# HGRN2 attention and a low-rank mixer on one core: the first batch's low rank in two groups of columns, and another order of loads around the last unit

## The chip, the cores and the metric

The kernel runs on 1 core of one Trainium2 chip. The metric is the device time of one execution in microseconds (us); lower is better. The profile, the chains and the timelines come from one profiled execution of the kernel.

## The reference

Two blocks follow each other, in float32 (the mixer's weights arrive as float64). For each of 4 batches and 8 heads (768 steps, head size 48) a gated linear recurrence is computed; the heads' outputs side by side make x, and a mixer works on it.

```python
f = 1 / (1 + exp(-f_logit))
for t in range(768):
    state = f[t][:, None] * state + k[t][:, None] * v[t][None, :]
    y[t] = q[t] @ state
x = heads of y side by side            # (4, 768, 384)
u = x + V.T @ (U.T @ x)                # along the sequence: U 768 x 32, V 32 x 768
out = u + relu(u @ w_ch1) @ w_ch2      # 384 -> 1536 -> 384
```

## The kernel before

**Units.** Two heads of one batch make a unit; there are HP = 4 units a batch and 16 in all. A unit takes a 96-column share of x (two heads of 48). `prepare(n)` makes the pieces of a unit's front: gates (f is transposed by TensorE and put through a sigmoid), keep (a scan on VectorE), keys, read_back (a second scan), queries. `attend(n)` makes those of its rear: kept, states (the ds matmuls), scan, scores (sc), read (the y matmuls from the states, L824), inner (the y matmuls within a chunk, L842, and the ScalarE copy of y into x, L848).

**Order.** TensorE (PE), VectorE (DVE) and ScalarE (ACT) run in the order in which the pieces are called; this order is written out by hand. The loop at L928 runs over the four units of the first batch and calls a front and a rear in turn. After it come the last unit's read and inner, then the first batch's mixer: low_rank (U.T x, tile ph, L172), added_up (the four 32-row groups of ph are summed by a matmul with `blocks`, L180), mix (V.T h added to x, tile pu, L197), turn (x transposed, tile put, L207), then the first large matmuls (pz, L219). `busy(n)` issues n matmuls whose result nobody reads (tile idle, L923).

**Loads.** All DMAs are issued by SyncE (SP), whose queue a scheduler orders by the calls and the waits of each. `load(n, names)` brings a unit's operands: f, k and q go into fixed tiles, `late` for even units and `other` for odd ones, each in two DMAs of 144 KB made of pieces of 192 bytes; v goes into one of three v_nat buffers with one DMA of 144 KB and two of 72 KB. `follow`, called as soon as a unit's f, k or q has been read, loads the same operand of unit n + 2 (for the first batch, units 2 and 3; units 4 and 5 are excepted). The loop's end adds the rest:

```python
            if n < 2:
                load(n + 2, "v")
            if n == 1:
                for start, _ in weights[: early + 2]:
                    start()
            elif n > 1:
                load(n + 2, "f", "k", "q", "v")
```

Each entry of `weights` is a pair: `start` issues the DMA of 8-byte values and `end` converts them to float32 (two ACT operations, three of DVE, one of POOL, L90 to L95). The first `early` = 3 are U and V (in two parts), then come twelve pieces of w1, the first FIRST = 6 of which land in spare zw tiles by `place`, the others in one of RAW = 4 w_raw buffers, and twelve of w2. `ahead_by(n, loads)` makes calls of which each starts the load n places further on and ends its own. The ends are called between the mixer's pieces; from piece EARLY on, pieces of the next batch's units are called between them too.

Of the kernel before, what the change touches and what calls it, by code (L numbers as in the profile page):

```python
# [10 lines left out]
F32 = mybir.dt.float32  # L11
U32 = mybir.dt.uint32
U64 = mybir.dt.uint64
I32 = mybir.dt.int32
AF = mybir.ActivationFunctionType
ALU = mybir.AluOpType
AX = mybir.AxisListType

WP = 384

RAW = 4
# [80 lines left out]
def ahead_by(n, loads):  # L102


    def call(i):
        if i + n < len(loads):
            loads[i + n][0]()
        loads[i][1]()

    return [lambda i=i: call(i) for i in range(len(loads))]  # L110
# [36 lines left out]
class Mixer:  # L147
# [6 lines left out]
    def __init__(self, tc, b, x, U, V, w1, w2, sums, ident, blocks, out, two, three, zp, ps_big, ps_mm, wide=False,  # L154
                 z_all=None, room=None, pair=0):
        nc = tc.nc
        P = nc.NUM_PARTITIONS
        NCH, DM = x.shape[1], x.shape[2]
        R, FF = U.shape[2], w1.shape[2]
        NG = P // R  # L160
        NDC, NFC = DM // P, FF // P
# [3 lines left out]
        uT, z, h, S = {}, {}, {}, {}  # L165

        def low_rank():
            pm = ps_mm.tile([P, 512], F32, name="ph", tag="mm")

            for c in range(NCH):  # L170
                g = slice((c % NG) * R, (c % NG + 1) * R)
                nc.tensor.matmul(pm[g, 0:DM], lhsT=U[:, c, :], rhs=x[:, c, :],  # L172
                                 start=(c < NG), stop=(c >= NCH - NG))
            h[0] = two.tile([P, DM], F32, name="h", bufs=1)
            nc.scalar.copy(h[0], pm[:, 0:DM])

        def added_up():

            pm = ps_mm.tile([P, 512], F32, name="ph", tag="mm")
            nc.tensor.matmul(pm[:, 0:DM], lhsT=blocks, rhs=h[0], start=True, stop=True)  # L180
            h[1] = two.tile([P, DM], F32, name="h", bufs=1)
            nc.scalar.copy(h[1], pm[:, 0:DM])

        def add(*args):

            with tc.high_priority(offset=AHEAD):
                nc.vector.tensor_tensor(*args)  # L187

        pu = {}

        def mix(t):

            s = t % 2
            if s == 0:
                pu[0] = ps_big.tile([P, 2, 512], F32, name="pu", tag="big")
            g = slice((t % NG) * R, (t % NG + 1) * R)
            nc.tensor.matmul(pu[0][:, s, 0:DM], lhsT=V[g, t // NG, :], rhs=h[1][g, :], start=True, stop=True)  # L197
            if s == 1:
                add(x[:, t - 1 : t + 1, :], x[:, t - 1 : t + 1, :], pu[0][:, :, 0:DM], ALU.add)

        def turn(a):

# [231 lines left out]
def factored_path(ctx, tc, q, k, v, f_logit, moe_U, moe_V, moe_w_ch1, moe_w_ch2, out, ok):  # L434
# [4 lines left out]
    nc = tc.nc  # L439
    B, H, S, D = q.shape  # L440
    P = nc.NUM_PARTITIONS
    C = P // 2
    NCH = S // C

    NBL = S // P
    HP = H // 2
    DM = H * D
    R = moe_U.shape[1]
    FF = moe_w_ch1.shape[1]
    NDC = DM // P  # L450
    NFC = FF // P
# [15 lines left out]
    two = ctx.enter_context(tc.tile_pool(name="two", bufs=2))  # L467
    three = ctx.enter_context(tc.tile_pool(name="three", bufs=3))
    zp = ctx.enter_context(tc.tile_pool(name="zp", bufs=3))
    ps_big = ctx.enter_context(tc.tile_pool(name="ps_big", bufs=3, space=bass.MemoryType.PSUM))  # L470
# [8 lines left out]
    raw = [{nm: t[:, i, :] for i, nm in enumerate("fkq")} for t in (late, other)]  # L479
# [11 lines left out]
    def load(n, *names):  # L491

        b, hp = divmod(n, HP)
        for nm in names:
            if nm == "v":
                v_tiles[n] = three.tile([P, NBL, 2, D], F32, name="v_nat")
            for par in range(2):
                head = src[nm][b, 2 * hp + par]
                if nm == "v" and par:

                    for s in range(2):
                        nc.sync.dma_start(
                            out=v_tiles[n][(1 - s) * C : (2 - s) * C, :, par, :],
                            in_=head.rearrange("(c s p) d -> s p c d", s=2, p=C)[s],
                        )
                    continue
                if nm == "v" or n < TURNED:
                    dst = v_tiles[n] if nm == "v" else nat[n % 2][nm]
                    nc.sync.dma_start(out=dst[:, :, par, 0:D], in_=head.rearrange("(c p) d -> p c d", p=P))  # L509
                    continue  # L510
                head = head.rearrange("(c i) d -> i c d", i=NB)
                for part in range(2):
                    p0 = par * PAD + part * NB
                    n_ch = min(NB, D - part * NB)
                    nc.sync.dma_start(
                        out=raw[n % 2][nm][p0 : p0 + NB, :].rearrange("p (c d) -> p c d", d=NB)[:, :, 0:n_ch],
                        in_=head[:, :, part * NB : part * NB + n_ch],
                    )
# [9 lines left out]
    blocks = const.tile([P, P], F32, name="blocks")  # L528
# [33 lines left out]
    table = one.tile([P, 1], F32, name="table")  # L562
# [4 lines left out]
    U = const.tile([P, NBL, R], F32, name="U")  # L567
    V = const.tile([P, (NBL * R + P - 1) // P, P], F32, name="V")
    take_in = weight_loader(nc, two, nc.sync)
    weights = [take_in(U, moe_U.rearrange("(c p) r -> p c r", p=P))]  # L570
    weights += [take_in(*pair) for pair in by_rows(V, moe_V, R)]
    early = len(weights)
    w1_rows = moe_w_ch1.rearrange("(c p) f -> p c f", p=P)

    spare = []

    def place():
        if not spare:
            t = zp.tile([P, NFC // 2, 2 * P], F32, name="zw").rearrange("p i t -> p (i t)").bitcast(U64)
            spare.extend([t[:, 0:WP], t[:, WP : 2 * WP]])  # L580
        return spare.pop(0)

    FIRST = 6
    weights += [
        take_in(w1[:, :, i * P : (i + 1) * P], w1_rows[:, :, i * P : (i + 1) * P], place if i < FIRST else None)
        for i in range(NFC)
# [96 lines left out]
    def mixer(b):  # L683
        return Mixer(tc, b, x_tiles[b], U, V, w1, w2, sums if b else None, ident, blocks, out, two, three, zp, ps_big, ps_mm,
                     b == 0, z_all, room if b >= B - 2 else None, FEWER - (b - B + 2) * NCH // 4)
# [180 lines left out]
    def rear(n, *names):  # L866

        if not 0 <= n < NU:
            return []
        if n not in here:  # L870
            here[n] = dict(zip(("kept", "states", "scan", "scores", "read", "inner"), attend(n)))
        return [here[n].pop(nm) for nm in names if nm in here[n]]
# [43 lines left out]
    with tc.manual_schedule(engines={nc.vector.engine, nc.scalar.engine}):  # L916


        idle = ps_mm.tile([P, 512], F32, name="idle", tag="mm")

        def busy(n):
            for _ in range(n):
                nc.tensor.matmul(idle[:, 0:DM], lhsT=ident, rhs=ends[:, 0:DM], start=True, stop=True)  # L923

        busy(1)
        for piece in front(0, "gates"):
            piece()
        for n in range(HP):  # L928
            pieces = front(n, "keep", "keys") + rear(n - 1, "scan", "scores")
            pieces += [lambda: busy(3)] + rear(n, "kept") + front(n, "read_back", "queries")  # L930
            if n + 1 < HP:
                pieces += front(n + 1, "gates") + rear(n - 1, "read", "inner") + rear(n, "states")
            else:
                pieces += rear(n, "states") + rear(n - 1, "read") + rear(n, "scan", "scores") + rear(n - 1, "inner")
            for piece in pieces:
                piece()
            if n < 2:
                load(n + 2, "v")
            if n == 1:


                for start, _ in weights[: early + 2]:
                    start()
            elif n > 1:
                load(n + 2, "f", "k", "q", "v")
        for start, _ in weights[early + 2 : early + FIRST]:
            start()
        loads = ahead_by(early + FIRST, weights)
        for piece in rear(HP - 1, "read") + loads[:2] + rear(HP - 1, "inner") + loads[2 : early + 1]:
            piece()  # L950
        loads = loads[early + 1 :]

        m = mixer(0)
        start = m.before[:5] + m.firsts[0:1] + m.before[5:]
        idles = {1: 1, 2: 1}

        EARLY = 9
        second = chain(front(HP, "gates", "keep", "keys", "read_back", "queries"), steps(HP, 2 * HP + 1))
        for i, (_, piece) in enumerate(start + m.firsts[1:]):
            busy(idles.get(i, 0))  # L960
            piece()
            if loads and i != 1:
                loads.pop(0)()
            if i >= EARLY:
                next(second)()
        for f in loads:
            f()
        n = len(m.seconds) // (NBL // 2)
        todo, after = m.seconds[:-n], m.seconds[-n:]

        attention(second, 12 + 10 * HP - (len(start) + len(m.firsts) - 1 - EARLY), todo)
        m = start_mixer(1, after)
        for f in to_sum:
            f()
    for b in range(2, B - 1):
        todo, after = m.main, m.after
        attention(steps(b * HP + 1, (b + 1) * HP + 1), 10 * HP, todo)
        m = start_mixer(b, after)

    pieces = beside(steps((B - 1) * HP + 1, NU + 1), 10 * (HP - 2), [lambda i=i: sum_of_w(i) for i in range(len(W_SUMS))])  # L980
# [374 lines left out]
```

## Time and profile before

| | us |
|---|---|
| median of 14 runs | 490.58 (488.65 to 494.15) |
| the profiled execution | 490.05 |
| its span | 488.3 |
| PE busy in the span | 471.3 (97%) |
| DVE busy | 356.2 (73%) |
| ACT busy | 163.6 (34%) |
| POOL busy | 36.4 (7%) |
| first large matmul of the mixer (pz) starts at | 57.31 |
| HBM read | 28.70 MB |

The page divides the span into 40 slices of 12.2 us and gives each engine's busy tenths in each. Its chain follows the work that ended last back from the end. A busy PE is not PE at its peak: a matmul's duration also depends on the clock that was granted to it, which the page shows in tenths (PEclk). "Issue" is time in which an engine waited for nothing that the profile shows.

### The profile page before, as it was taken

The numbers are of one execution on the slowest core, as the hardware profiler recorded it, in microseconds if no ns is written. First come the engines' busy times: TensorE is split into PE (matmuls) and PEld (weight loads), VectorE is DVE, ScalarE is ACT, GpSimd is POOL, SyncE is SP. The second block draws the span as 40 slices with busy tenths as digits, with TensorE's granted clock in tenths as the row PEclk, the third lists the DMA queues.
The fourth block names the chain that finished last, engine by engine and source line by source line (L and its number), as shares of the span: only waits on it lengthen the run. The fifth ranks groups of instructions, "written<-read, shape, count | busy, mean of one in ns | idle before, by whom it ended". The sixth has DMA issues, their size and how long they took to land.

```text
span 488.3 us, 12681 instructions
## 1 busy us (share of the span) xinstructions
PE 471.3 (97%) x5519; PEld 400.4 (82%) x5519; DVE 356.2 (73%) x561; ACT 163.6 (34%) x307; POOL 36.4 (7%) x49
## 2 busy tenths in 40 slices
PE   7897999999999999999999999999999999999995
PEld 4675588886666568899899888898979999999995
DVE  5886789778998757656857448796896886958642
ACT  3444575654443313424231403432231312112200
POOL 3001255442000000000000000000000000000000
PEclk9998899999999999999999999999999999999999
DMA  9988976675778512333434100100000000000001
GB/s 145 159 175 157 260 181 154 158 155 66 110 108 128 91 37 33 56 44 79 66 52 85 34 17 17 27 3 20 18 2 0 34 2 16 17 1 34 0 34 38
DMA packets 158679, 34.34 MB, mean 70 GB/s; under 512 B 149206, under 2 KB 157078, under 8 KB 158614
## 3 DMA queue, kind: packets, MB, share of 16 engines
q1 hardware_dynamic: 158614, 33.44, 37.3%
q8 instruction: 45, 0.74, 0.6%
q14 instruction: 20, 0.16, 0.1%
HBM read 28.70 MB, written 4.72 MB: 68 GB/s over the span
## 4 chain that ended last, share of the span: by engine, by line
PE 90%; DVE 3%; DMA 2%; SPq 2%; issue 1%; ACT 1%; DVEq 0%; ACTq 0%
PE pw L273 26%; PE pz L219 23%; PE pp L371 11%; PE po L244 10%; PE y L824 3%; PE y L842 3%; PE sc L749 3%; PE ds L786 2%; PE pt L621 2%; PE put L207 2%; PE pt L770 1%; PE idle L923 1%; SPq L509 1%; PE pu L197 1%; PE ph L172 1%
## 5 line engine op out<-in xcount | busy, mean ns | idle before, releaser
L219 PE MATMUL pz<-uT,w 128*128 128x256 f32 x504 | 115.8, 384 | 0.1
L219 PEld LDWEIGHTS pz<-uT,w 128*128 128x128 f32 x504 | 93.3, 190 | 13.3 <-issue 0.3
L273 PE MATMUL pw<-w,z_all 128*128 128x192 f32 x216 | 37.7, 329 | 0.0
L273 PE MATMUL pw<-zw,w_raw 128*128 128x192 f32 x216 | 37.4, 327 | 0.0
L273 PEld LDWEIGHTS pw<-zw,w_raw 128*128 128x128 f32 x216 | 35.2, 190 | 0.8 <-issue 0.6
L273 PEld LDWEIGHTS pw<-w,z_all 128*128 128x128 f32 x216 | 35.0, 190 | 0.7
L655 DVE TENSOR_TENSOR_SCAN late<-fz,late 128x768 f32<-128x768 f32 x16 | 28.1, 1756 | 9.8 <-ACT fz L650 5.1
L95 POOL TENSOR_TENSOR w<-w_y,w_r 128x384 int32<-128x384 int32 x24 | 30.2, 1258 | 37.0 <-DVE w_y L94 30.0
L229 ACT ACTIVATE z_all<-pz 128x512 f32<-128x512 f32 x33 | 19.7, 596 | 39.6 <-PE pz L219 39.5
L371 PE MATMUL pp<-v_nat,late 128*128 128x128 f32 x224 | 28.8, 275 | 0.0
L673 DVE TENSOR_TENSOR_SCAN late<-fz,other 128x768 f32<-128x768 f32 x16 | 27.9, 1746 | 0.1
L371 PEld LDWEIGHTS pp<-v_nat,late 128*128 128x128 f32 x224 | 27.0, 192 | 0.0
L244 PE MATMUL po<-w,zw 128*128 128x384 f32 x72 | 25.6, 499 | 0.0
L244 PE MATMUL po<-w,z_all 128*128 128x384 f32 x72 | 25.3, 496 | 0.0
L364 ACT ACTIVATE other<-other 128x512 f32<-128x512 f32 x18 | 11.3, 631 | 40.0 <-DVE other L187 40.0
L812 ACT COPY st<-added 128x576 f32<-128x576 f32 x12 | 14.7, 1224 | 26.0 <-DVE added L807 26.0
L756 DVE TENSOR_TENSOR A<-sc,causal 128x768 f32<-128x768 f32 x16 | 15.2, 948 | 10.1 <-PE sc L749 10.1
L92 DVE TENSOR_SCALAR w_y<-w_y 128x384 f32<-128x384 f32 (+3 forms) x27 | 11.8, 438 | 11.8 <-ACT w_y L90 11.6
L244 PEld LDWEIGHTS po<-w,zw 128*128 128x128 f32 x72 | 12.9, 189 | 8.7 <-issue 1.2
L244 PEld LDWEIGHTS po<-w,z_all 128*128 128x128 f32 x72 | 13.1, 190 | 8.5 <-DVE o L187 0.6
L187 DVE TENSOR_TENSOR w_raw<-z_all 128x768 f32<-128x768 f32 x12 | 11.5, 955 | 10.6 <-ACT z_all L229 9.2
L842 PEld LDWEIGHTS y<-v_nat,A 64*64 64x64 f32 x768 | 13.3, 137 | 7.1 <-issue 5.4
(185 smaller groups left out, 835.2 us busy)
## 6 DMA issues: line engine op xcount, KB each, us to landing
w_raw<-in_moe_w_ch_dram SPq DMA_DIRECT2D x18, 384.0 KB, 3.9
out_dram<-o SPq DMA_DIRECT2D x24, 192.0 KB, 1.9
v_nat<-in_v_dram SPq DMA_DIRECT2D x16, 144.0 KB, 3.3
v_nat<-in_v_dram SPq DMA_DIRECT2D x32, 72.0 KB, 3.0
zw<-in_moe_w_ch_dram SPq DMA_DIRECT2D x6, 384.0 KB, 5.8
late<-in_f_logit_dram SPq DMA_DIRECT2D x10, 96.0 KB, 3.6
late<-in_k_dram SPq DMA_DIRECT2D x10, 96.0 KB, 2.7
late<-in_q_dram SPq DMA_DIRECT2D x10, 96.0 KB, 2.6
```

The lines of the kernel that those rows point to most:

```text
L95: nc.gpsimd.tensor_tensor(dst.bitcast(I32), shaped(y.bitcast(I32)), shaped(r), ALU.add)
L219: nc.tensor.matmul(pm[:, i * 2 * P : (i + 1) * 2 * P], lhsT=w1[:, m, o : o + P], rhs=uT[a][:, m, :], start=(m == 0), stop=(m == NDC - 1))
L229: nc.scalar.activation(z[a, c][:, k : k + 2, :].rearrange("p i t -> p (i t)"), pm, AF.Relu)
L244: nc.tensor.matmul(pm, lhsT=z[a, i // NI][:, i % NI, s * P : (s + 1) * P], rhs=w2[:, i, :], start=(i == 0), stop=(i == NFC - 1))
L273: nc.tensor.matmul(pm[:, n * HM : (n + 1) * HM], lhsT=lhs[:, i, :], rhs=rhs[:, i, :], start=(i == 0), stop=(i == NI - 1))
L371: nc.tensor.matmul(pm[:, i, r * P : (r + 1) * P], lhsT=room["w"](wn)[:, r * P : (r + 1) * P], rhs=x_node(a, xn), start=((xn, wn) == of[0]) ...
L655: nc.vector.tensor_tensor_scan(backwards(X, S - 1, S), backwards(f, S, S), backwards(ends, S - 1, S), 0.0, ALU.mult, ALU.add,)
L673: nc.vector.tensor_tensor_scan(Y, f[:, 0:S], starts, 0.0, ALU.mult, ALU.add)
L749: nc.tensor.matmul(sc[part[s ^ par], par, c * C : (c + 1) * C], lhsT=T["k"][rows[par], chunk[2 * c + s]], rhs=T["q"][rows[par], chunk[2 * ...
L756: nc.vector.tensor_tensor(T["A"], sc[:, :, 0 : NBL * C].rearrange("p h (c i) -> p h c i", i=C), causal.unsqueeze(1).unsqueeze(1).broadcast ...
L812: nc.scalar.copy(st, states.rearrange(by_e, c=NCH))
L842: nc.tensor.matmul(o(s, par, c), lhsT=T["A"][part[s ^ par], par, c, :], rhs=vt[part[s ^ par], c, par, :], start=False, stop=True, skip_gro ...
```

## The change

- The four-unit loop no longer calls the last unit's rear; it is written out after the loop, with the ends of the first weights (U, V, w1's first two pieces) between its pieces.
- In the last round of the loop (n = 3) the operands of unit 5 aren't loaded any more; they are loaded later, after the first part of the low rank. The condition becomes `elif n < HP - 1`. With HP = 4 this branch ran for n = 2 and 3 before; it runs for n = 0 and 2 after (n = 1 takes the branch above it).
- The first batch's low rank, sum and addition to x are computed in two groups of columns: the 288 of units 0 to 2 (`done`) and the 96 of unit 3 (`rest`). The low rank of `done` stands between the last unit's read and its inner product. The 12 ph matmuls become 12 of 288 columns and 12 of 96, the sum becomes two, and x is added to in five DVE operations in place of three. They use the ps_big PSUM tiles. h gets two buffers.
- Two one-element copies on ACT read the first element of a spare zw tile and of unit 5's f place, after the copy of the first ph; loads into these two places wait for them. The element of the zw tile is set to zero by POOL at the start. The six spare places of zw are taken when the program begins.
- The four `busy` matmuls in the mixer's start go, and EARLY is 6 in place of 9 (the list of pieces is three shorter).

```diff
+        def low_rank_of(cols):
+            pm = ps_big.tile([P, 2, 512], F32, name="ph", tag="big")[:, 0]
+            for c in range(NCH):
+                g = slice((c % NG) * R, (c % NG + 1) * R)
+                nc.tensor.matmul(pm[g, cols], lhsT=U[:, c, :], rhs=x[:, c, cols],
+                                 start=(c < NG), stop=(c >= NCH - NG))
+            if not hs:
+                for i in range(2):
+                    hs[i] = two.tile([P, DM], F32, name="h", bufs=2)
+            nc.scalar.copy(hs[0][:, cols], pm[:, cols])
+
+        def added_up_of(cols):
+            pm = ps_big.tile([P, 2, 512], F32, name="ph", tag="big")[:, 0]
+            nc.tensor.matmul(pm[:, cols], lhsT=blocks, rhs=hs[0][:, cols], start=True, stop=True)
+            nc.scalar.copy(hs[1][:, cols], pm[:, cols])
+
+        def mix_of(cols):
+            n = cols.stop - cols.start
+            share = 2 * n <= 512
+            for t in range(0, NG if share else NCH, 2):
+                ...
+                        nc.tensor.matmul(pm[:, s, k, :], lhsT=V[g, i // NG, :], rhs=hs[1][g, cols], start=True, stop=True)
+                ...
+                add(xv, xv, pm, ALU.add)
...
+    FIRST = 6
+    for _ in range(FIRST // 2):
+        t = zp.tile([P, NFC // 2, 2 * P], F32, name="zw").rearrange("p i t -> p (i t)")
+        spare.extend([t[:, 0 : 2 * WP], t[:, 2 * WP : 4 * WP]])
+    held = [spare[2][:, 0:1], raw[1]["f"][:, 0:1]]
+    nc.gpsimd.memset(held[0], 0.0)
...
             if n + 1 < HP:
                 pieces += front(n + 1, "gates") + rear(n - 1, "read", "inner") + rear(n, "states")
-            else:
-                pieces += rear(n, "states") + rear(n - 1, "read") + rear(n, "scan", "scores") + rear(n - 1, "inner")
             for piece in pieces:
                 piece()
             if n < 2:
                 load(n + 2, "v")
             if n == 1:
                 for start, _ in weights[: early + 2]:
                     start()
-            elif n > 1:
+            elif n < HP - 1:
                 load(n + 2, "f", "k", "q", "v")
+
+        done, rest = slice(0, 2 * n * D), slice(2 * n * D, DM)
+        ends_of = [end for _, end in weights]
+        pieces = rear(n, "states") + rear(n - 1, "read") + rear(n, "scan") + ends_of[:1] + rear(n, "scores")
+        pieces += ends_of[1:2] + rear(n - 1, "inner") + rear(n, "read") + ends_of[2 : early + 1]
+        for piece in pieces:
+            piece()
+        m = mixer(0)
+        low_rank_of, added_up_of, mix_of = m.some
+        low_rank_of(done)
+        for t in held:
+            nc.scalar.copy(table, t)
         for start, _ in weights[early + 2 : early + FIRST]:
             start()
-        loads = ahead_by(early + FIRST, weights)
-        for piece in rear(HP - 1, "read") + loads[:2] + rear(HP - 1, "inner") + loads[2 : early + 1]:
+        load(n + 2, "f", "k", "q", "v")
+        for start, _ in weights[early + FIRST : early + FIRST + RAW]:
+            start()
+        ends_of[early + 1]()
+        for piece in rear(HP - 1, "inner"):
             piece()
-        loads = loads[early + 1 :]
-        m = mixer(0)
-        start = m.before[:5] + m.firsts[0:1] + m.before[5:]
-        idles = {1: 1, 2: 1}
-        EARLY = 9
+        added_up_of(done)
+        low_rank_of(rest)
+        mix_of(done)
+        added_up_of(rest)
+        mix_of(rest)
+        loads = ahead_by(FIRST - 2 + RAW, weights[early + 2 :])
+        start = m.before[3:5] + m.firsts[0:1] + m.before[5:]
+        EARLY = 6
         second = chain(front(HP, "gates", "keep", "keys", "read_back", "queries"), steps(HP, 2 * HP + 1))
         for i, (_, piece) in enumerate(start + m.firsts[1:]):
-            busy(idles.get(i, 0))
             piece()
-            if loads and i != 1:
+            if loads:
                 loads.pop(0)()
```

## The prediction

> **What bounds the kernel now.** I read the page's busy times and slices first. They say where TensorE (PE) isn't full.
>
> ```profile
> PE 471.3 (97%) x5519; PEld 400.4 (82%) x5519; DVE 356.2 (73%) x561; ACT 163.6 (34%) x307; POOL 36.4 (7%) x49
> ...
> PE   7897999999999999999999999999999999999995
> ...
> PEclk9998899999999999999999999999999999999999
> DMA  9988976675778512333434100100000000000001
> ```
>
> A slice is 12.2 us. From the sixth on (61 us) PE is full, and the page's chain is 90% PE. So whatever moves the first large matmul (pz, 57.31 us) moves the end one for one. The first four slices are different: PE below 9, DMA at 9 or 8. Next, the chain of waits there (start, us, what):
>
> ```profile
> 14.61 5.31 DMA late<-in_f_logit_dram
> 19.92 0.14 issue
> 20.05 0.85 PE pt L621 x6
> 20.90 1.19 PE y L824 x44
> ```
>
> The transposes of unit 2's f (pt L621, 20.05) start 0.13 us after that f lands: PE runs only just behind the loads. Then SP's timeline of DMA issues (start, us from the first issue to the end of the last, count):
>
> ```profile
> 14.03 1.13 SPq L509 DMA_DIRECT2D late<-in_f_logit_dram  x2
> ...
> 22.35 2.40 SPq L502 DMA_DIRECT2D v_nat<-in_v_dram  x2
> 24.85 1.15 SPq L509 DMA_DIRECT2D other<-in_k_dram  x2
> 26.10 2.26 SPq L509 DMA_DIRECT2D other<-in_q_dram  x2
> 28.46 0.49 SPq L509 DMA_DIRECT2D v_nat<-in_v_dram  x1
> ```
>
> SP needs until 24.75 us to issue unit 2's f, k, q, unit 3's f and unit 2's v, and the queue is never far ahead. Last, the chain where batch 0's mixer starts:
>
> ```profile
> 43.59 0.25 PE y L842
> 43.85 1.45 issue
> 45.30 1.32 PE y L842 x47
> 46.62 0.02 issue
> 46.64 0.65 ACT x L848
> 47.29 0.14 issue
> 47.42 2.77 PE ph L172 x12
> 50.20 1.58 PE idle L923 x2
> 51.78 1.05 PE ph L180 x2
> 52.83 0.65 PE idle L923 x2
> 53.47 0.01 issue
> 53.49 0.93 PE pu L197 x8
> ```
>
> From the end of unit 3's read (43.36) to the first put (55.45) 12.1 us go by in series: inner product, x copy, low rank, sum, part of x. From 45.8 to 52.6 the windows view shows a granted clock of 0.50, which is why the ph took 2.77 us; the same twelve took 1.48 us at 163 us.
>
> **What the Trainium skill says.** "TensorE: Matmul & The Clock Gate", Part 1: an idle PE falls to half clock, and about 3.4 us of sustained work brings it back. The trace agrees: 0.50 for 6.8 us after the 1.45 us hole at 43.85. "DMA: Bandwidth & Descriptors", Specifications: transfers reach line rate only from 512 B. The trace agrees: these loads move 192 B pieces, and the windows show 154 to 178 GB/s between 8 and 24 us against 348 at 57 to 61 us, where weights move. Same page, Two DMAs through the same engine are not ordered: only the completion semaphore tells that data has landed, so a reader must wait for the last load into its buffer. That decides step 1.
>
> **The change, part by part.** The sum is made against the profiled execution's own 490.05 us (span 488.3 and 1.75 around it), which lies 0.53 below the runs' median of 490.58.
>
> 1. *The condition of the whole-unit load.* `elif n > 1` becomes `elif n < HP - 1`. With HP = 4 it now also holds at n = 0: load(2, f, k, q, v) runs although `follow` has already loaded unit 2's f, k and q, and the line above its v. In the built order SP gets 9 DMAs more (2 f, 2 k, 2 q, 3 v; 6 x 144 + 144 + 2 x 72 = 1152 KB), just behind unit 2's first v and ahead of unit 3's k. The order of PE waits shows that unit 2's f transposes no longer wait for the first pair of f loads but for the second. So gates(2), at 20.05 us before, needs an f that SP can't issue before 24.75. The pair takes the place that unit 3's k had: issued at 24.85 and 25.45. Landing: the first v of unit 2 landed at 27.17 by the trace, and a 144 KB load goes through in 0.9 us (19.01, 19.92, 20.82 are the landings of three in a row), so two more end at 29.0; the second route is the q issued at 26.10, landed at 30.30, less 0.9 for one load earlier, 29.4. PE starts 0.13 later: 29.1 to 29.5 against 20.05. **Plus 9.3 us** (9.0 to 9.7), with nothing to hide it: PE is in order, and read(0), inner(0), states(1) and unit 2's k are queued behind; ACT, DVE wait for PE. The rest of the second copy is in time: k at 31.1 (needed at 33.2 after the shift), q at 32.9 (37.5), v at 34.7 (41.2), unit 3's k at 36.5 (42.0), all at 0.9 a load. U, V and the first w1, issued behind, gain distance from their users, since these shift by 9 as well.
>
> 2. *Half clock after that hole.* PE is idle for 10.7 us from 18.8. By the trace's own case it restarts at 0.50 and needs 3.4 to 6.8 us. The pieces after it: pt 0.85, y 1.19, y 0.92, ds 0.70, pt 0.81, sc 0.86, idle 2.13. Short matmuls stretch by 1.32/0.91 = 1.45 (47 of y L842, half against full clock): 3.66 us in the first four cost 1.6 more; up to sc 2.4; were the idle ones doubled too, 4. **Plus 2.0** (0 to 4).
>
> 3. *The mixer's start.* Removed: the 12 ph of 384 columns after the last x copy and four idle matmuls there. Added: 12 ph of 288 columns (1.48 x 0.75 = 1.1) ahead of unit 3's inner product, where PE otherwise waited for `seen`; afterwards 12 ph of 96, two sums instead of one, 6 pu of 288 columns and 6 of 96 for 6 of 384, five x additions on DVE instead of three (128x768 took 0.97; 576, 576, 576, 384, 192 elements: 2.9 for 2.68), two copies of one element on ACT (0.2 each), a POOL memset of one column at the start (free, 0.1). On ACT the x copy now stands behind V's second part, w1's first two pieces and the h copy: from 43.56 that is 0.55 + 0.3 (wait for POOL) + 1.0 + 0.4 + 0.4 + 1.0 + 0.65 for the copy, so x ends at 47.85 before the shift against 47.29. Then ph of 96 (0.4), pu 0.9, additions, second sum, pu, put: about 51.2 for the first put and 52.9 for the first pz, against 55.45 and 57.31: minus 4.4 at full clock. But PE has holes there (45.4 to 47.9 nearly empty) and no idle matmuls, so the clock may be halved when pz starts, at 2.6 us for twelve: up to 3.4 back. **Minus 3.4** (4.4 to 1.0).
>
> 4. *The hold.* w1_2 and half of unit 5's f wait on SP for the ACT copies after the first h (46.2 before the shift); behind them in SP's order are unit 5's second v, w1_6 to w1_9. w1_2 takes 4.0 to 7.5 us (the zw loads' range), landing at 50.2 to 53.7; ACT comes to its conversion after the first uT copy, at 52.5. **Taken as 0**, 1.2 at worst, and then uT and the relu behind it are late. It could also gain: w1 then no longer shares the rings with U; I give nothing. Unit 5's f isn't needed before 86.8.
>
> 5. *Later order.* One w2 conversion moves a piece later on ACT and DVE (2.6 us); POOL ended at about 117 and the last quarter of po starts at 121.8: covered by 2 us. Nothing.
>
> Sum: 490.05 + 9.3 + 2.0 - 3.4 = **498.0**. Bounds: 490.05 + 9.0 + 0 - 4.4 = 494.7; 490.05 + 9.7 + 4.0 - 1.0 + 1.2 = 504.0.
>
> **Rivals.** (a) *The mixer's gain wins*: it would be 490.05 - 4.4 = 485.7, faster. Mechanism: the second copy of unit 2 isn't gating, because f needn't be awaited or lands before 20.05 + the gain, that is before about 24.5. The point is there: the reload decides from a landing of 24.5 on. For it speaks only that PE had 0.6 + 1.45 us of issue holes to lose too; against it, SP's 24.75. 4%. (b) *The hold becomes the bound*: ACT waits for w1_2 the full 1.2, pz runs at half clock for 6.8 us (3.4 lost), cold restart 4: 490.05 + 9.3 + 4.0 - 1.0 + 1.2 = 503.5. For it: four idle matmuls gone; against: two windows of busy pz should suffice. 18%. (c) *The change does little*: the reload is hidden for 5 us and the gain meets it, 490: it needs DMA at twice the rate seen. 3%. The forecast: 75%.
>
> **Numbers.** Forecast and (b) give a slower kernel, 93%; (c) 3%; (a) 4%. About 0.3% (1.5 us) is what a measurement can tell here from no change. The range reaches from just under the forecast's lower bound, run scatter taken in, to (b).
>
> **What would show it.** Right: HBM read rises from 28.70 to 29.9 MB; pt L621 of unit 2 waits for DMA late for 10 us and starts near 29.4; the third slice of PE falls; put starts near 63 instead of 55.5; from there the two timelines run parallel. Step 2: a clock of 0.50 after 29 us. Wrong: gates(2) still at 20, or a put within 2 us of 55.5.

## The result, and the profile after

The changed kernel takes 502.79 us (median of 10 runs, 501.62 to 504.28), against 490.56 for the kernel before in the same session (47 runs): ratio 1.0252, 95% interval 1.0232 to 1.0273. The profiled execution took 501.56 us (before 490.05) with a span of 499.8 (before 488.3), so the traces differ by 11.5 us.

The page's busy times, slices, clock and DMA rows, kernel after:

```profile
PE 473.0 (95%) x5541; PEld 403.4 (81%) x5541; DVE 355.7 (71%) x563; ACT 163.2 (33%) x311; POOL 37.3 (7%) x50
...
PE   7569789999999999999999999999999999999995
...
PEclk9959899999999999999999999999999999999999
DMA  9999875667467732340723410100000000000001
...
HBM read 29.88 MB, written 4.72 MB: 69 GB/s over the span
```

PE is busy 1.7 us longer, in a span that is 11.5 longer. What is new stands in slices 2 and 3 (12 to 37 us): PE falls to 5 and 6, and the clock of the third slice to 5. HBM read rises by 1.18 MB, the nine loads. From the seventh slice on the PE rows agree. SP's timeline of issues, kernel after (start, us, count):

```profile
14.24 1.14 SPq L548 DMA_DIRECT2D late<-in_f_logit_dram  x2
...
23.79 1.20 SPq L548 DMA_DIRECT2D late<-in_f_logit_dram  x2
...
31.15 1.16 SPq L548 DMA_DIRECT2D other<-in_k_dram  x2
```

Unit 2's f is loaded at 14.24 and again at 23.79; unit 3's k, issued at 24.85 before, now goes at 31.15. The chain of waits there, kernel after:

```profile
24.45 4.49 DMA late<-in_f_logit_dram
...
29.07 1.51 PE pt L665 x6
30.59 1.47 PE y L868 x44
```

The transposes of unit 2's f (pt, now L665) start at 29.07 in place of 20.05, and take 1.51 in place of 0.85 us. The windows view of the stretch, kernel after (window, length, then busy us of PE, PEld, DVE, ACT, POOL, then granted clock, DMA share, GB/s):

```profile
34.00:36.00 2.00, 2.00 (x49) 1.91 (x42) 0.00 (x0) 1.28 (x3) 0.00 (x0) 0.50 0.70 129
36.00:38.00 2.00, 2.00 (x52) 1.60 (x51) 1.39 (x2) 0.00 (x0) 0.00 (x0) 0.65 1.02 193
```

The clock is 0.50 in every window from 24 to 36, and full again from about 37.4 (worked out from the mean of 0.65 over 36 to 38). Last, the chain where the mixer starts, kernel after:

```profile
56.73 1.10 PE ph L208 x2
57.83 1.46 issue
59.29 1.17 PE ph L208 x10
...
62.09 0.53 ACT x L892
...
68.58 2.83 PE pz L258 x12
```

From the end of unit 3's read (56.73; 43.36 before) to the first pz (68.58; 57.31 before) it is 11.85 us in place of 13.95. Between these two profiles the order of the mixer's start thus gains 2.1 us, and the 1.45 us of "issue" that stood in the inner product is now in the low rank.

### The profile page after: what moved, and what is told of

Same layout as the page of the kernel before. It is cut to its first block, busy times and chain, and to the rows that moved or that the text cites. A ratio compares the mean times of both kernels' runs of the same rounds, so it can differ in the third digit from the quotient of the medians.

```text
span 499.8 us, 12743 instructions
## 1 busy us (share of the span) xinstructions
PE 473.0 (95%) x5541; PEld 403.4 (81%) x5541; DVE 355.7 (71%) x563; ACT 163.2 (33%) x311; POOL 37.3 (7%) x50
## 4 chain that ended last, share of the span: by engine, by line
PE 75%; DVE 11%; DMA 4%; SPq 4%; issue 3%; ACT 2%; DVEq 0%; ACTq 0%
PE pw L312 25%; PE pz L258 20%; PE pp L410 11%; PE pt L665 2%; PE y L868 2%; PE sc L793 2%; PE y L886 2%; PE idle L967 2%; PE ds L830 2%; DVE late L717 2%; PE po L283 2%; DMA late<-in_f_logit_dram 2%; PE put L246 1%; SPq L548 1%; PE pt L814 1%
## 5 line engine op out<-in xcount | busy, mean ns | idle before, releaser
L312 PE MATMUL pw<-zw,w_raw 128*128 128x192 f32 x216 | 37.4, 327 | 0.0
L92 DVE TENSOR_SCALAR w_y<-w_y 128x384 f32<-128x384 f32 (+3 forms) x27 | 13.1, 484 | 15.2 <-ACT w_y L90 15.0
L665 PE MATMUL pt<-ident,late 128*128 128x128 f32 x54 | 10.3, 343 | 10.7 <-DMA late<-in_f_logit_dram 10.4
```

The source lines that it names most:

```text
L312: nc.tensor.matmul(pm[:, n * HM : (n + 1) * HM], lhsT=lhs[:, i, :], rhs=rhs[:, i, :], start=(i == 0), stop=(i == NI - 1))
L665: nc.tensor.transpose(pt[:, 2 * c // NBL, c % (NBL // 2) * P : (c % (NBL // 2) + 1) * P], nat[n % 2][nm][:, c].rearrange("p h d -> p (h d) ...
```

## The experiments

Two theories were to be told apart: that the loss is **a wait** of unit 2's f transposes for the second copy (with the half clock after it), or that it is **the volume** of 1152 KB more on queues that are full. Beside them stood the question where the mixer's gain went.

**No second copy.** The condition is narrowed, and the rest of the change stays.

```diff
-            elif n < HP - 1:
+            elif 1 < n < HP - 1:
```

> Everything of the change is kept but the condition, which becomes 1 < n < HP - 1, so that unit 2 is loaded once. Theory (the second copy of unit 2 costs 12.2 us at the start of unit 3's rear: 9.0 of waiting for f and 3.2 of half clock after it; the new order around the mixer gains about 2): gates(2) is back at 20 us, pz starts near 55, time about 488.4 (490.56 - 2.1), HBM read 28.70 MB. The prediction's own step 3 would give 487.1. Rival (the new order itself is slow: the hold and the missing idle matmuls): 492 or more, pz later than 57.3.

Measured: 490.48 us against 489.96, ratio 1.0002 (0.9976 to 1.0029). The loss is gone with the second copy, but no gain is left either: the theory's 488.4 was missed by 2.1 us. Its timeline of PE at the first large matmuls shows why:

```profile
56.34 2.83 PE L258 MATMUL pz<-uT,w 128*128 128x256 f32 x12 [0.33 <-ACT uT L247]
...
60.77 2.86 PE L258 MATMUL pz<-uT,w 128*128 128x256 f32 x12 [0.95 <-ACT uT L247]
63.92 5.45 PE L258 MATMUL pz<-uT,w 128*128 128x256 f32 x24 [0.29 <-ACT uT L247]
```

pz starts 1.0 us earlier than before (57.31), but its 48th ends at 69.37 against 68.71. The uT copies that it waits for stand on ACT behind the conversion of w1's third piece, and this waits for its load, in the chain of the same kernel:

```profile
55.04 3.91 DMA zw<-in_moe_w_ch_dram
```

The hold's two copies on ACT were done at 48.8. SP issues the load only at 55.04, because it stands in SP's queue behind unit 5's k, q and v, whose issue took from 47.4 to 54.9.

**The second copy alone**, in the kernel before.

```diff
-            elif n > 1:
+            elif n > 1 or n == 0:
```

> The kernel before with one edit: the whole-unit load also runs at n = 0. Theory: the second copy costs the same without the rest of the change: gates(2) near 29.1, unit 3's kept 12.2 us later than before, and the time 502.8 to 504 (490.56 + 12.2, and up to 1.2 more where the mixer starts). Rival (the loss comes from the new order): below 494.

Measured: 501.51 us, ratio 1.0213 (1.0164 to 1.0262). One condition makes nearly the whole loss, though the median of its four runs is 1.3 us below the range expected. (Where the expectations speak of unit 3's `kept` or rear as 12.2 us late, unit 2's is meant.) In its timeline of PE the bracket is the wait ahead of the group:

```profile
28.70 1.51 PE L621 MATMUL pt<-ident,late 128*128 128x128 f32 x6 [9.54 <-DMA late<-in_f_logit_dram]
```

**The same nine loads to another place.** They stand at the same place in SP's queue and read the same bytes, but land in a tile that nobody reads at that time.

```diff
-            elif n < HP - 1:
-                load(n + 2, "f", "k", "q", "v")
+            elif 0 < n < HP - 1:
+                load(n + 2, "f", "k", "q", "v")
+            elif n == 0:
+                ...  # unit 2's f, k, q, v by nine DMAs into z_all
```

> The changed kernel with the nine extra DMAs at the same place in SP's queue and of the same shape, but landing in a tile that nobody reads then (z_all). It tells waiting for the second copy from carrying it. Theory (the wait decides): gates(2) starts near 20 as before; what is left is that unit 3's k lands near 35.7, 3.0 us after TensorE wants it (32.7), and up to 2 us of half clock; with the gain of 2.1 the time is 491.5 to 493.5. Rival (the 1.15 MB on a full DMA queue is the cost): about 502.8 as with the change.

Measured: 495.64 us, ratio 1.0105 (1.0073 to 1.0136). Its chain:

```profile
32.69 4.20 DMA other<-in_k_dram
...
37.02 1.51 PE pt L665 x6
```

Unit 2's f is in time again (pt at 19.93), but unit 3's k, behind the nine loads, comes 4.3 us late (pt at 37.02; before 32.68), with half clock after it. Neither theory named the time: the first was 2.1 us too low, because the half clock cost 2.9 us and not up to 2 (from that pt to the transposes of `kept` 6.83 us, 3.92 before) and came back at put and pz (57.20 to 64.03). So the bytes alone cost 5.1 us against the kernel without them (490.48). They can't be set beside the 9.0 us as a share: in the change unit 3's k arrives under the shift that the wait for f makes.

**Only f twice.**

```diff
-                load(n + 2, "f", "k", "q", "v")
+                load(n + 2, *("f" if n == 0 else "fkqv"))
```

> The changed kernel, in which the additional load of unit 2 brings only f again (2 DMAs of 144 KB in place of 9 of 1152 KB). If the loss is the wait of unit 2's f transposes for the second f (theory), they start between 28 and 29.5 us as in the changed kernel, at half clock, and the kernel takes 500 to 503. If it is the volume of the nine loads (rival), they start near 21 to 22 and it takes 491 to 494.

Measured: 502.35 us, ratio 1.0228 (1.0184 to 1.0271), the same as with all nine. Its chain:

```profile
23.93 4.26 DMA late<-in_f_logit_dram
...
28.32 1.51 PE pt L665 x6
```

Two loads of 144 KB are enough. With the run before, which shows what the bytes cost without the wait, this settles the first question: the wait on the second f sets the loss of the change; the other seven loads are hidden behind it.

**A warm wait.** A call of `busy(13)` fills PE's wait for that f (its 13 matmuls are 26 in the trace, two for each).

```diff
+                pieces += [lambda: busy(13)] if n == 1 else []
                 pieces += front(n + 1, "gates") + ...
```

> The changed kernel with 13 idle matmuls of 384 columns (about 0.71 us each at full clock, 9.2 in all) ahead of unit 2's f transposes, in the hole where TensorE waits for the second copy of f. Theory: the wait of 9 us stays, the half clock after it goes: unit 3's kept is 9.0 us later than before and not 12.2, time 499.6. Rival (the half clock is hidden behind VectorE's scans, and the 12.2 is all waiting for loads): unchanged, 502.8.

Measured: 498.93 us, ratio 1.0211 (1.0149 to 1.0273). This interval overlaps that of the change (1.0232 to 1.0273), so the runs alone don't show a gain; the trace does. In the chain:

```profile
28.21 0.85 PE pt L665 x6
29.06 1.19 PE y L868 x44
```

With the clock at 1.00 in every window from 24 to 34 us, unit 2's pieces from the f transposes to the transposes of `kept` take 8.2 us (28.21 to 36.41), against 10.9 in the change (29.07 to 39.96) and 7.7 before (20.05 to 27.74). Half clock is thus worth at least 2.7 of the 3.2 us that unit 2's pieces took longer in the change; of what is left over here, 0.36 is an "issue" among the transposes of k. The load of w1's third piece stands in the chain here too (61.46 to 65.95; the uT copy at 70.16), though the pz behind it waited only 0.26 us.

**No hold**, in the kernel without second copy.

```diff
-    held = [spare[2][:, 0:1], raw[1]["f"][:, 0:1]]
-    nc.gpsimd.memset(held[0], 0.0)
+    held = []
```

> The changed kernel without the second copy of unit 2 and without the two one-element copies that hold loads back (so the order and the column groups of the mixer's start alone). If the hold ate the gain of the mixer's start (theory), w1's third piece is there in time, pz starts near 56.3 and runs through without the holes of 2.9 and 0.3 us: about 1.0 to 2.5 below before, 487.5 to 489. If the order itself gains nothing (rival), it stays within 0.3% of before, 489.5 to 491, with pz starting at 57 or later.

Measured: 488.97 us against 490.55, ratio 0.9958 (0.9938 to 0.9978). Its timeline of PE:

```profile
54.84 2.83 PE L258 MATMUL pz<-uT,w 128*128 128x256 f32 x12 [0.32 <-ACT uT L247]
...
58.16 7.94 PE L258 MATMUL pz<-uT,w 128*128 128x256 f32 x36
```

All of pz runs through, and its 48th ends at 66.10, 2.6 us ahead of before. SP issues w1's third piece with the pieces around it, by 47.4, ahead of unit 5's loads. pz starts 1.5 us earlier than with the hold. That part isn't the hold's: it lies in the low rank, which ran at half clock there (2.14 us for eleven ph) and at full clock here (1.18). So of the 3.3 us between the two profiles at the 48th pz, the hold accounts for about 1.8; the medians differ by 1.5.

**Only half of unit 5's f held.**

```diff
-    held = [spare[2][:, 0:1], raw[1]["f"][:, 0:1]]
-    nc.gpsimd.memset(held[0], 0.0)
+    held = [raw[1]["f"][:, 0:1]]
```

> As the kernel without second copy and hold, but half of unit 5's f is still held back. The theory that only w1's third piece matters says the same time as without any hold, 487.5 to 489; if crowding of the DMA rings by unit 5's f is what the hold protects from, this one is faster than that without any hold by 0.5 us or more.

Measured: 488.76 us, ratio 0.9960 (0.9938 to 0.9983), the same as with no hold. Of the two copies, the one on w1's third piece cost the gain; of that on f the runs show neither cost nor gain.

**The change without the hold**, second copy included.

> The changed kernel, second copy of unit 2 included, without the two one-element copies that hold loads back. In the changed kernel's trace w1's third piece landed at 64.75 us and ACT came to it at 68.4, so the hold should cost nothing there: 502 to 503.5 (theory). If the hold also cost about 2 us in the change (rival), 500 to 501.

Measured: 503.23 us, ratio 1.0253 (1.0181 to 1.0326). The four runs lie between 501.07 and 507.54, too far apart to exclude the rival's 500 to 501, and their trace has a hole of its own (below). What decides is the trace of the change: there SP was through with the loads of unit 5 that stand ahead at 59.1, before ACT's copies came (61.0); it issued w1's third piece at 61.03, which landed at 64.75, and ACT came to it at 68.3, after the uT copy. The load was in time by 3.6 us, and the hold cost the 0.2 us of its two copies on ACT at most (60.88 to 61.10 in the chain). The trace without the hold has an "issue" of 3.62 us among the low rank's matmuls, where most of the others have 0.8 to 2.2; from the end of unit 3's read to the first pz it takes 14.5 us, not 11.85. What sets the length of this hole stays open.

**w1's second piece elsewhere on ACT.** In the kernel with neither second copy nor hold, the conversion of w1's second piece (1.0 us of ACT) stands ahead of the last x copy. It was put behind this copy, then behind the copies of the sum and of the second low rank, then there again with three calls of `busy(1)` in PE's holes.

```diff
-        ends_of[early + 1]()
         for piece in rear(HP - 1, "inner"):
             piece()
+        ends_of[early + 1]()          # first kernel: here
         added_up_of(done)
         low_rank_of(rest)
         mix_of(done)
+        ends_of[early + 1]()          # second and third kernel: here
+        busy(1)                       # third kernel alone, and behind
         added_up_of(rest)             # each of these two calls again
         mix_of(rest)
```

> As the kernel without second copy and hold, and the end of w1's second piece (two ACT operations of 1.0 us together) stands behind the last x copy in place of ahead of it. If ACT's queue sets the last x copy (theory), x comes 0.7 to 1.0 us earlier, and so does the first pz: 0.5 to 1.0 below the kernel without hold, near 487.5. If the inner product on PE sets it (rival), nothing changes; if w1's second piece becomes late for the second group of pz, it is slower by up to 1.

> As the kernel without second copy and hold, with the end of w1's second piece (1.0 us of ACT) behind the copies of the first sum and of the second low rank, ahead of the copy of the second sum only. The place behind the x copy alone gave its 0.8 us back at the sum's copy; here ACT has a hole of 1.5 us. Theory: the last x copy and the second low rank come 0.5 us earlier and nothing behind them is late, 488.4 or a little less. Rival: w1's second piece is now late for pz, or the second sum's copy is: 489 to 490.

> As the one before, with one idle matmul in each of three holes of PE in the mixer's start (0.3 us each, holes of 0.33 to 0.36 us). If half clock at put and pz (1 us lost in two of four profiles) is what remains, 488.0 or 0.3 to 0.5 below the one without them; if the idle matmuls only delay what follows, 0.3 above.

Measured: 489.93 us (ratio 0.9987, 0.9975 to 1.0000), 490.43 (0.9991, 0.9971 to 1.0011) and 488.80 (0.9962, 0.9944 to 0.9981). None is clearly ahead of 488.97: the third is level with it (ratios 0.9962 and 0.9958), the first two came out slower. Both theories by which an earlier x gives a faster kernel failed. The timelines of PE, first and second kernel:

```profile
50.62 1.24 PE L233 MATMUL pu<-h,V 32*128 32x288 f32 x12 [0.76 <-ACT h L213]
```

```profile
55.76 2.40 PE L246 MATMUL put<-ident,x 128*128 128x128 f32 x10 [1.20 <-DVE x L187]
57.95 4.60 PE L258 MATMUL pz<-uT,w 128*128 128x256 f32 x12
```

In the first, PE no longer waits for the x copy ahead of the second low rank, but 0.76 us for ACT ahead of pu: the wait moved one step on. In the second, DVE's part of the same conversion stands ahead of the second addition to x (1.20 us), and after that hole twelve pz take 4.60 in place of 2.83 us at half clock. (This profiled execution, 492.53 us, lies 2.1 above the median of its kernel, so not every run loses that much.) The third fills its holes (a `busy(1)` took 0.67 to 0.84 us, not the 0.3 of the expectation) and has a clock of 1.00 in every window from 40 to 68 us; its pz takes 2.83 again. The ratios' intervals of the last two overlap a little (0.9971 to 1.0011, 0.9944 to 0.9981), so that the idle matmuls are worth 1.6 us is likely, not shown beyond doubt.

The best kernels thus have neither the second copy nor the hold on w1: 488.97 and 488.76 us, and 488.80 with w1's second piece behind and the holes filled, all about 0.4% under before.

## Why the prediction was right or wrong

The side, the mechanism and the range held; the value came out 4.8 us under the median. Set against the two profiled executions, the steps stand so:

| step | forecast | measured | from |
|---|---|---|---|
| 1, wait for the second f | +9.3 | +9.0 | pt at 29.07 and 20.05 |
| 2, half clock after it | +2.0 | +3.2 | the idle matmuls ahead of unit 2's `kept` at 37.82 and 25.61, less 9.0 |
| not foreseen, unit 3's scores and the reads around them | 0 | +1.2 | end of read at 56.73 and 43.36, less 12.2 |
| 3, mixer's start | -3.4 | -2.1 | first pz at 68.58 and 57.31, less 13.4 |
| 4 and 5 | 0 | +0.2 | the rest to 11.5 |
| sum | +7.9 | +11.5 | 501.56 and 490.05 |

*Step 1* was right in cause and size. The landing at 28.9 lies a little under the two routes of the prediction (29.0 and 29.4); the copy alone and f alone show that nothing else is needed for it. That it fits so closely is in part luck: SP issued the second half of f at 24.45, not at 25.45, because unit 2's v took it less time, and that half needed 4.49 us to land, where the two routes allow 3.6 to 4.0. (Where the prediction says that PE is below 9 in the first four slices, the third is at 9; nothing rests on it.)

*Step 2* was mis-sized twice. The stretch of 1.45, taken from one form of matmul, isn't common to all: the first pt took 1.51 for 0.85 (1.8), the y of the inner product 1.53 for 0.92 (1.7), ds 1.28 for 0.70 (1.8), y from the states 1.47 for 1.19 (1.2). And the half clock lasted 8.3 us from the restart at 29.07, not the 3.4 to 6.8. The Trainium skill ("TensorE: Matmul & The Clock Gate", Part 1) gives about 3.4 us of sustained work, and says that the window in which work is measured is free-running: it does not start with the work. The traces agree. Apart from the end of the kernel, every stretch of half clock in the 13 of them is one, two or four times 3.41 us long. In the change it is four, from 23.76 to 37.41 (kernel after, columns as above):

```profile
23.76:27.17 3.41, 0.00 (x0) 0.00 (x0) 0.00 (x0) 0.00 (x0) 0.00 (x0) 0.50 0.96 165
27.17:30.58 3.41, 1.51 (x10) 1.21 (x12) 0.00 (x0) 0.00 (x0) 0.00 (x0) 0.50 1.08 157
30.58:34.00 3.42, 3.16 (x109) 3.00 (x112) 2.18 (x4) 1.14 (x4) 0.00 (x0) 0.50 0.88 161
34.00:37.41 3.41, 3.41 (x82) 2.99 (x78) 0.80 (x1) 1.28 (x3) 0.00 (x0) 0.50 0.84 159
```

PE restarts within the second, still waits 0.26 us for ACT (`seen`) in the third, and is busy throughout only in the fourth; then the clock is full. The prediction counted from the restart, and as if any work were enough. The 6.8 us that it read in the kernel before are two such windows (45.63 to 52.46), and there too PE was busy throughout only in the second. The bounds (0 to 4) did hold it.

*The term that was missing*: the windows from 54 to 58 have a clock of 0.62 and 0.53 once more, after 1.26 us of "issue" at 52.43 (0.58 there before). About 0.7 of the 1.2 us is that longer hole; the rest is mostly the inner product of unit 2 and the read of unit 3 at half clock (1.12 and 1.20 us in the chain, 0.70 and 1.02 before). The prediction looked for half clock behind the long wait and at pz, not between them.

*Step 3* had the right pieces, but left the 1.45 us of "issue" in the inner product out of the new order without a reason, and reckoned the last x copy from ACT's queue alone: 4.5 us after the read. It ended at 62.62, 5.9 after it, because the hole is now among the ph (57.83, 1.46 us) and the h copy, w1's second piece and the x copy all queue behind those. The fear for pz was not met in the change, where the first twelve took 2.83 us, but that is the luck of one profile: of the ten other kernels with the new order, five show them at 3.41 to 4.60 us.

*Step 4*, the hold at nothing, was right for the change, as its own trace shows; the runs without the hold scatter too much to add to it. The reason given was too weak, though: it took w1's third piece as issued when ACT's copies are done. SP is in order, and in the kernel without second copy it is still busy with unit 5's loads for 6.2 us after that (48.8 to 55.0). There the hold is the bound and takes the gain away. *Step 5* was not tested alone; behind the first pz the two profiles differ by 0.2 us.

*Rival (b)* named nearly the right time (503.5) for reasons that don't hold: w1's third piece was not awaited in the change and pz ran at full clock; only its cold restart (4, measured 3.2) was near. *Rival (a)* is refuted twice: f was awaited, and without the second copy the gain is 1.8 us at best (488.76 against 490.55), not 4.4. *Rival (c)* would have needed the reload hidden for 5 us; it was not.

## What to carry to other kernels

A condition that is widened to reach one more round should be read for every round: here `n < HP - 1` in place of `n > 1` also took in round 0, and two loads of 144 KB into a buffer that already held the right data cost more than everything else in the change together, because its reader waits for the last load into it. When a wait is made for one load, look at what stands ahead of that load in the issuing queue: the wait ends when the queue comes to it, not when its condition is met. Where a hole on PE may bring half clock, reckon its end in whole windows (3.41 us here) up to the first that is full of work, price the short matmuls in them one form at a time, and look for where the next hole of "issue" will fall once the order changes.

## What the runs showed of the hardware that was not expected

- In these 13 traces half clock ended with the first window of 3.41 us in which PE was busy 93% or more; after windows with 92% or less it went on. In the change a wait of 0.26 us among short matmuls was all that the window from 30.58 to 34.00 lacked, and the half clock went on for 3.41 us more. With idle matmuls in the wait the clock was 1.00 in every window from 24 to 34 us (0.85 us for the six f transposes).
- What makes the clock fall is not settled by them. In the kernel before it fell after a window in which PE was busy for 1.70 of 3.41 us (42.22 to 45.63); in the kernel without second copy and hold it did not fall after one with 1.74 (43.80 to 47.21). So two profiles of nearly the same program can differ by a stretch of half clock.
- Small matmuls stretch by 1.2 to 1.8 at half clock, by form. The six long idle ones took 3.89 us with the nine loads elsewhere, against 2.13, and the last 0.4 us of them were at full clock again.
- Holes of "issue" on PE stand in bursts of many small matmuls. The 1.45 us in the inner product before went when the order changed, and most kernels with the new order have 0.8 to 3.62 us in the low rank that follows the same reads; with the loads elsewhere it was 0.19, and in the warm wait the hole stood in the read itself (1.24). Nothing in these traces tells what sets their length.
